# A gated mix of two long convolutions: one group moved back from the end to the middle of the run, the tap filter in wide multiplications, the gate by tanh

## The chip, the cores and the metric

One core of a Trainium2 chip. Its engines are PE (TensorE, matmuls; PEld is its loading of weights), DVE (VectorE), ACT (ScalarE), POOL (GpSimd) and SP (SyncE, which only issues DMAs here). Each has an in-order queue of its own, and they meet at semaphores. The metric is the device time of one execution in microseconds; the median of three runs is compared.

## The reference

```
g = sigmoid((u * gate_w).sum(-1, keepdims=True))
# A: a diagonal state space model as one long convolution per channel
K = einsum("dn,dnl,dn->dl", C, exp(dt * A * l), dt * B).real      # 448 channels, 256 modes, 2048 steps
a = causal_conv(u, K) + u * Dskip
# B: a gated convolution
k_shift = sum over t < 4 of k[s - t] * shift_k[:, t]              # the tap filter
kv = k_shift * v
b = u * (causal_conv(kv, ssm_k) + kv * ssm_D)
out = g * a + (1 - g) * b                                         # [1, 2048, 448], bf16
```

The convolutions are by FFT over 4096 points in the reference.

## The kernel before

**Layout.** The 2048 steps stand as 32 partitions of 64 steps, four times, once for each quarter of 112 of the 448 channels. So a tensor like `u`, `k` or `v` is a tile of 128 partitions x 64 x 112. The 112 columns are handled in four groups (`NQG = 4`, `NC = 28` columns each), for both convolutions: groups B0 to B3 and A0 to A3.

**One group.** A convolution is done as a Fourier transform by matmuls. `spread` (first stage, L215, PSUM tiles `ps_c`) and `transform` (second stage, L227, PSUM tiles `ps`) bring a tile `zs` into frequencies; each PSUM tile is brought to SBUF by a cast on ACT (`evac`, L567). A B group needs this for its filter (`KB`, from `skraw`) and for its data (`XB`, from `kv`); an A group for its data (`XA`, from `uu`) and for the generated kernel (`KA`, `zsK`). `swapped` (L605) makes a copy `zsS` with real and imaginary halves exchanged, by two DMAs on SP's queue. `products` (L286) multiplies both copies by the other factor, on DVE, two multiplications of 128x3584. `stage_a` (L265, `ps_a`, cast into `U`) and `stage_b` (L279, `ps_b`) transform back, and an epilogue on DVE puts the result into `ug`: L734 for B groups (`ug` holds u times 1-g by then), L744 and L746 for A groups. A2's result is held in `y` and mixed in later (`mix_y`, L764 and L765).

**The generated kernel.** K comes in eight blocks of 14 columns (`KGen.block(j)`, j = 0 to 7), two for each A group. A block is a chain of multiplications and additions on DVE that makes two tables of powers, `kg_TQ` and `kg_TP` (L320, L325, L330; the copy at L334 is among the first of each block), then 224 small matmuls `pk` (L373), a cast `kg_S` on ACT, a gather by matmuls (L414), two casts `kg_KT`, and a spread with `WcK` into `zsK`. Ahead of every second block `Tables.chunk(H)` makes the exponentials and phases for two blocks: ACT computes exponentials (L483, tiles `ks_mag` and `ET`) and sines (L495), which are in different tables, and DVE makes the phases (L491, `ks_ph`) and multiplies (L508). The queue order holds all sines of a chunk together and all exponentials together, by `after`.

**The front.** `k` is loaded into `kt` with three earlier steps ahead of it. The tap filter goes over 64 steps, eight at a time, from the last to the first: four multiplications on DVE (L653), each of eight steps of `kt` shifted by one step more, times that tap's row of `wt`, and then eight matmuls with the identity (L657), which add the four up in PSUM, and a cast back into `kt`. The matrices `A`, `B` and `C` come as `modes`, are transposed on PE (L447) and used at L436 and L455.

**The gate.** `ug` is first used for u times `gate_w` (L820), summed by matmuls (L823) and a reduction (L825); the sigmoid (L826) makes g in `gt`. `gb` holds g and `og` 1-g, and L832 makes `ug` = u times 1-g.

**The order.** `seq` says which group is convolved back in which step. `step(c, n, j)` brings in the next group n (spread, transform), takes the current group c back (stages A and B), and runs block j. A scheduler sets the order of instructions on each engine; `tc.high_priority` and `after` steer it. In this kernel B3 isn't in `seq`: its place is `None` (step 3 brings in nothing, step 4 takes nothing back), its spreads and transforms are written in the step of block 6, and its products, stages A and B come behind block 7. The last A group is done in two halves of 14 columns (`transform_half` L241, `last` L843, `stage_a_half` L253), each after one of the last two blocks; then stage B, the epilogue and the stores to `out` (L739).

Of the kernel before, what the change touches and what calls it, by code (L numbers as in the profile page):

```python
# [9 lines left out]
ACT = mybir.ActivationFunctionType  # L10
ALU = mybir.AluOpType
# [6 lines left out]
P = 128  # L18
# [4 lines left out]
NQG = 4  # L23
NC = 112 // NQG
CB = NC // 2
NBLK = 2 * NQG
# [25 lines left out]
def after(tc, ins, before):  # L52
    tc.add_manual_dep(ins.ins, before.ins.name,
                      mybir.DependencyInfo(mybir.DependencyClass.NoSync, mybir.DependencyReason.DATA),
                      reason="order on one engine")
# [6 lines left out]
class Consts:  # L62
# [67 lines left out]
    def stage_a(self, s_col, off_col):  # L130
        nc = self.nc
        j = self.iota("sa_j", [[1024, 64]])
        ph = self.carve(256).rearrange("p (i b) -> p i b", i=4)
        for i, off in enumerate((off_col[0][:, 0:1], off_col[1][:, 0:1], HALF, QUARTER)):
            self.phases(ph[:, i, :], j, s_col, off)
        R = self.pool.tile([P, 256], bf16, name="sa_R")
        nc.scalar.activation(R[:], low16(ph.rearrange("p i b -> p (i b)")), ACT.Sin, scale=PHASE)
        return R

    def stage_b(self, pool, qt, hqt, k_col, mask):  # L140
        nc = self.nc
        G = pool.tile([P, 64, 2, 4, 32], bf16, name="sb_G")
        jv = self.iota("sb_j", [[8, 16], [512, 32]]).rearrange("p (b a) -> p b a", b=16)
        offs = self.pool.tile([P, 4, 2], f32, name="sb_offs")
        for b0 in range(0, 64, 16):
            ph = qt([P, 16, 2, 32], "sb_ph", i32)
            for r, turn in enumerate((QUARTER, HALF)):
                o = offs[:, b0 // 16, r:r + 1]
                nc.vector.tensor_scalar(out=o, in0=k_col[:], scalar1=8.0 * b0, scalar2=turn, op0=ALU.mult, op1=ALU.add)
                self.phases(ph[:, :, r, :], jv, k_col, o)  # L150
            v = pool.tile([P, 16, 2, 32], bf16, name="sb_v", tag="kg_P4", bufs=2)
            nc.scalar.activation(v[:].rearrange("p b r a -> p (b r a)"), low16(ph[:].rearrange("p b r a -> p (b r a)")),
                                 ACT.Sin, scale=PHASE)
            for g in range(4):
                nc.vector.tensor_scalar(out=G[:, b0:b0 + 16, :, g, :], in0=v[:], scalar1=mask[:, g:g + 1], scalar2=None, op0=ALU.mult)
        return G
# [64 lines left out]
def transform(nc, psum, W, zs, evac, ks=range(4)):  # L221
    n = 4 * NC
    for kk in ks:
        pt = psum.tile([P, 2, 512], f32, name="ps_2", tag="ps")
        for i in range(8):
            k = 8 * kk + i
            nc.tensor.matmul(pt[:, i // 4, (i % 4) * n:(i % 4 + 1) * n], lhsT=W[:, k].rearrange("p r s -> p (r s)"), rhs=zs[:, k],  # L227
                             start=True, stop=True)
        evac(zs[:, 8 * kk:8 * kk + 8].rearrange("p (i k) c -> p i (k c)", i=2), pt[:, :, 0:4 * n], kk % 2)
# [50 lines left out]
        consume(b0, n, pt[:, :, 0:448])  # L280


def products(nc, X, S, Y, behind=None, k0=0, k1=32):
    fl = lambda t: t[:, k0:k1].rearrange("p k c -> p (k c)")
    for t in (S, X):
        op = nc.vector.tensor_tensor(out=fl(t), in0=fl(t), in1=fl(Y), op=ALU.mult)  # L286
        if behind is not None:
            behind(op)
    return X, S


# [236 lines left out]
def body(  # L528
# [20 lines left out]
    nc = tc.nc  # L549
    V = nc.vector  # L550
# [8 lines left out]
    qp = ctx.enter_context(tc.tile_pool(name="qp", bufs=NBQ))  # L559
    psum = ctx.enter_context(tc.tile_pool(name="psum", bufs=3, space=PSUM))  # L560
# [17 lines left out]
    def qt(shape, name, dtype=bf16):  # L578
        return qp.tile(shape, dtype, name=name, tag="q")
# [17 lines left out]
    def spread_in(cols):  # L597
        zs = qt([P, 32, 4 * NC], "zs")
        spread(nc, psum, Wc, zs, cols, [list(range(j, min(j + 8, NC))) for j in range(0, NC, 8)], evac)
        return zs  # L600

    def swapped(zs, op=None):
        swap = qt([P, 32, 4 * NC], "zsS")
        for r in range(2):
            d = nc.sync.dma_start(swap[64 * r:64 * r + 64], zs[64 - 64 * r:128 - 64 * r])  # L605
            if op is not None:
                behind_other(tc, d, op)
        return zs, swap

    kt = kgp.tile([P, 67, 112], bf16, name="kt", tag="kg_E")  # L610
# [4 lines left out]
    wraw = cons.carve(224).bitcast(bf16).rearrange("p (l t) -> p l t", t=4)  # L615
# [29 lines left out]
    ident = cons.carve(P // 2).bitcast(bf16)  # L645
    V.tensor_scalar(out=ident, in0=ji, scalar1=0.0, scalar2=None, op0=ALU.is_equal)
    wt = cons.carve(224).bitcast(bf16).rearrange("p (t l) -> p t l", t=4)
    wtc = nc.scalar.copy(wt, wraw.rearrange("p l t -> p t l"))
    for b0 in range(56, -1, -8):
        pt = psum.tile([P, 2, 512], f32, name="ps_v", tag="ps")  # L650
        t = qt([P, 4, 8, 112], "kvt")
        for n, tau in enumerate((3, 2, 1, 0)):
            V.tensor_tensor(out=t[:, n], in0=kt[:, b0 + 3 - tau:b0 + 11 - tau, :],  # L653
                            in1=wt[:, tau, :].unsqueeze(1).to_broadcast([P, 8, 112]), op=ALU.mult)
        for i in range(2):
            for n in range(4):
                nc.tensor.matmul(pt[:, i, 0:448], lhsT=ident, rhs=t[:, n, 4 * i:4 * i + 4, :].rearrange("p b l -> p (b l)"),  # L657
                                 start=(n == 0), stop=(n == 3))
        evac(kt[:, b0 + 3:b0 + 11, :].rearrange("p (i b) l -> p i (b l)", i=2), pt[:, :, 0:448])
# [4 lines left out]
    W2 = cons.stage_2(cons.field("b2", 0, 63), [cons.field("o2%d" % r, 6, 1, -QUARTER, (1 + r) * QUARTER) for r in range(2)], kgp, wtc)  # L664
    k_col, mask_b = cons.field("kB", 2, 31, 4.0, 1.0, pool=wp), cons.onehot("mgB", 4, cons.field("gB", 0, 3), 1.0 / 2048, pool=wp)
    R = cons.stage_a(cons.field("sA", 0, 63), [cons.field("oA%d" % r, 6, 1, HALF, (1 - r) * QUARTER) for r in range(2)])
    tb = Tables(tc, kgp, qt, hqt, psum, raw, ident, dt, xfd, nc.sync)
    tb.coefficients()
    G = cons.stage_b(kgp, qt, hqt, k_col, mask_b)
# [97 lines left out]
    def kv_cols(H):  # L767
        return lambda c: kvq[H][:, :, c]
# [1 line left out]
    def u_cols(H):  # L770
        return lambda c: uu[:, :, H * NC + c]

    def consume_a(c):
        with tc.high_priority(offset=300000):
            return stage_a(nc, psum, qp, R, terms[c], evac)

    def consume_b(c, U):
        with tc.high_priority(offset=200000):
            stage_b(nc, psum, G, U, (hold_y if c == ("A", NQG - 2) else epilogue_A if c[0] == "A" else epilogue_B)(c[1]))

    def step(c, n, j):
        kind, H = n if n else (None, None)
        if kind == "B":
            KB[H] = spread_in(skc.pop(H))
            XB[H] = spread_in(kv_cols(H))
        elif kind == "A":
            XA[H] = spread_in(u_cols(H))
        if c:
            U = consume_a(c)
        if kind == "B":  # L790
            transform(nc, psum, W2, KB[H], evac)
            transform(nc, psum, W2, XB[H], evac)
        elif kind == "A":
            transform(nc, psum, W2, XA[H], evac)
        if j == NBLK - 2:
            KB[3] = spread_in(skc.pop(3))
            XB[3] = spread_in(kv_cols(3))
            transform(nc, psum, W2, KB[3], evac)
            transform(nc, psum, W2, XB[3], evac)
        if c:  # L800
            consume_b(c, U)
        if kind == "B" and H + 1 < NQG:
            skc[H + 1] = sk_cols(H + 1)
        block(j)
        if kind == "B":
            with tc.high_priority(offset=200000):
                terms[n] = products(nc, *swapped(KB[H], kg.summed), XB[H])
        elif kind == "A":
            XA[H] = swapped(XA[H], kg.summed)
        if kind == "A" and H < NQG - 1:  # L810
            transform(nc, psum, W2, KA[H], evac)
            with tc.high_priority(offset=200000):
                terms[n] = products(nc, *XA[H], KA[H])
# [9 lines left out]
        nc.tensor.matmul(pg[:], lhsT=ones[:], rhs=ug[:, :, l:l + 8], start=(l == 0), stop=(l == 104))  # L823
    gt = wp.tile([P, 64], f32, name="gt")
    V.tensor_reduce(out=gt[:], in_=pg[:], op=ALU.add, axis=mybir.AxisListType.X)  # L825
    nc.scalar.activation(gt[:], gt[:], ACT.Sigmoid)  # L826
    gb = wp.tile([P, 64, 2], bf16, name="gb")
    V.tensor_copy(gb[:], gt[:].unsqueeze(2).to_broadcast([P, 64, 2]))
    og = wp.tile([P, 64, 2], bf16, name="og")
# [1 line left out]
    pairs = lambda t: t[:].rearrange("p b (n t) -> p b n t", t=2)  # L831
    V.tensor_tensor(out=pairs(ug), in0=pairs(uu), in1=og[:].unsqueeze(2).to_broadcast([P, 64, 56, 2]), op=ALU.mult)  # L832

    seq = [("B", 0), ("B", 1), ("B", 2), ("A", 0), None, ("A", 1), ("A", 2), ("A", 3)]
    for j in range(NBLK - 1):
        step(seq[j], seq[j + 1], j)

    KB[3] = swapped(KB[3], kg.summed)

    def last(half):  # L840
        for k0 in (0, 16):
# [3 lines left out]
    transform_half(nc, psum, W2, KA[3], evac, 0)  # L845
    last(0)
    block(NBLK - 1)
    terms["B", 3] = products(nc, *KB[3], XB[3], lambda op: after(tc, op, kg.last))
    consume_b(("B", 3), consume_a(("B", 3)))
    U = qt([P, 2, 64, NC], "U")  # L850
    transform_half(nc, psum, W2, KA[3], evac_two, 1)
    stage_a_half(nc, psum, U, R, XA[3], evac, 0)
    last(1)
# [38 lines left out]
```

## Time and profile before

| | us |
|---|---|
| median of three runs | 343.5 (341.89 to 343.77) |
| the profiled execution, its own time | 341.89 |
| its span, first to last instruction | 340.1 |
| busy: DVE / ACT / PE / PEld / POOL | 277.0 / 243.6 / 228.9 / 199.4 / 32.4 |
| mean granted TensorE clock | 0.817 |

The span is what the profile's rows lie in; the execution's own time is 1.8 us more. Starts are from the span's start. A row's duration has some 0.05 to 0.1 us that overlap the next row on the same engine, so sums over many instructions are made from start to start.

### The profile page before, as it was taken

Reading aid. Unit: us, or ns where it says so; the run is one execution under the profiler, and the core shown is the slowest. Engines: PE = TensorE matmul, PEld = TensorE weight load, DVE = VectorE, ACT = ScalarE, POOL = GpSimd, SP = SyncE. Lnnn points to the kernel's source line nnn. Section 1 sums busy time; section 2 is a strip of 40 time slices with the busy share of each in tenths; the row PEclk is TensorE's granted clock in tenths of the full one; section 3 lists DMA queues with packets and bytes.
Section 4 is the critical chain, followed back from the end, with each engine's and each line's share of the span. In section 5 each row is a group of like instructions: output and inputs, shape, how many; then the busy total and the mean of one; then the engine's idle time right before and its main releaser. Section 6 shows DMA issues by size and latency. Waiting matters only on the chain.

```text
span 340.1 us, 11947 instructions
## 1 busy us (share of the span) xinstructions
PE 228.9 (67%) x5286; PEld 199.4 (59%) x5286; DVE 277.0 (81%) x571; ACT 243.6 (72%) x395; POOL 32.4 (10%) x129
## 2 busy tenths in 40 slices
PE   0598325845497587799827887939759949847740
PEld 0145325345386486698717776839649848747740
DVE  7899999977997999799999999999999930171640
ACT  2745978599954899979768597889846837874320
POOL 9300003720000073000000000000000000000000
PEclk9999965678587679589958759678969997996995
DMA  5889999430002410500310100400040040400038
GB/s 112 141 186 154 162 164 194 165 54 0 2 2 57 90 24 5 150 2 4 83 30 4 44 3 5 110 0 4 16 95 5 4 110 4 110 2 0 4 76 142
DMA packets 53740, 21.41 MB, mean 63 GB/s; under 512 B 49080, under 2 KB 52024, under 8 KB 53688
## 3 DMA queue, kind: packets, MB, share of 16 engines
q1 hardware_dynamic: 48936, 19.47, 30.1%
q10 hardware_dynamic: 4560, 1.15, 1.9%
q8 instruction: 41, 0.67, 0.9%
q14 instruction: 11, 0.09, 0.1%
q0 software_dynamic: 192, 0.03, 0.1%
HBM read 10.09 MB, written 3.21 MB: 39 GB/s over the span
## 4 chain that ended last, share of the span: by engine, by line
DVE 40%; ACT 28%; PE 12%; SPq 6%; DMA 4%; issue 3%; POOL 3%; DVEq 0%; ACTq 0%
DVE kg_P L320 10%; ACT zs L567 9%; ACT ET L483 5%; PE ps_b L279 4%; ACT U L567 4%; DVE zs L286 3%; DVE zsS L286 3%; DVE kg_TQ L325 3%; DVE kg_TP L330 3%; DVE ks_ph L491 3%; DVE kg_TP L325 3%; POOL skraw L594 3%; ACT ks_mag L483 2%; PE pk L373 2%; PE ps_a L265 2%
## 5 line engine op out<-in xcount | busy, mean ns | idle before, releaser
L567 ACT CAST zs<-ps_c 128x1024 bf16<-128x1024 f32 (+1 forms) x48 | 41.6, 923 | 5.6 <-PE ps_c L215 5.6
L320 DVE TENSOR_TENSOR kg_P<-kg_TQ,ET 128x896 bf16<-128x896 bf16 (+1 forms) x64 | 43.8, 706 | 0.4
L227 PEld LDWEIGHTS <-s_W 128*128 128x128 bf16 x480 | 33.8, 117 | 16.1 <-issue 13.8
L567 ACT CAST zs<-ps 128x896 bf16<-128x896 f32 x48 | 40.7, 932 | 2.2 <-PE ps L227 2.2
L265 PE MATMUL ps_a<-sa_R,zs 128*128 128x128 bf16 x196 | 33.2, 263 | 12.1 <-DVE zs L286 7.8
L373 PE MATMUL pk<-kg_TP,kg_TQ 128*21 128x32 bf16 x1792 | 30.2, 238 | 12.1 <-issue 8.5
L227 PE MATMUL ps<-zs,s_W 128*128 128x112 bf16 x384 | 30.2, 242 | 11.7 <-ACT U L567 6.0
L373 PEld LDWEIGHTS <-kg_TQ 128*21 128x21 bf16 x1792 | 27.8, 121 | 13.8 <-issue 13.1
L567 ACT CAST U<-ps_a 128x1024 bf16<-128x1024 f32 (+2 forms) x32 | 28.8, 938 | 9.6 <-PE ps_a L265 7.4
L265 PEld LDWEIGHTS <-zs 128*128 128x128 bf16 x196 | 28.2, 156 | 8.8 <-DVE zs L286 8.3
L265 PE MATMUL ps_a<-sa_R,zsS 128*128 128x128 bf16 x196 | 32.7, 261 | 0.0
L279 PE MATMUL ps_b<-U,sb_G 128*128 128x28 bf16 x1024 | 27.6, 177 | 5.5 <-ACT U L567 3.7
L279 PEld LDWEIGHTS <-sb_G 128*128 128x128 bf16 x1024 | 27.5, 98 | 6.4 <-issue 6.2
L215 PE MATMUL ps_c<-WcK,kg_KT 128*64 128x128 bf16 x224 | 19.1, 298 | 17.7 <-ACT zsK L567 13.0
L320 DVE TENSOR_TENSOR kg_P<-kg_TP,ET 128x1792 bf16<-128x1792 bf16 (+1 forms) x32 | 30.9, 965 | 0.0
L265 PEld LDWEIGHTS <-zsS 128*128 128x128 bf16 x196 | 28.2, 157 | 4.4 <-issue 4.3
L594 POOL TENSOR_TENSOR skraw<-skraw,dB 128x28 bf16<-128x28 bf16 x4 | 21.1, 5277 | 97.8 <-DMA skraw<-in_B_ssm_k_dram 71.1
L215 PEld LDWEIGHTS <-kg_KT 128*64 128x64 bf16 x224 | 16.6, 209 | 20.2 <-issue 14.8
L325 DVE TENSOR_TENSOR kg_TQ<-kg_P 128x896 bf16<-128x896 bf16 (+2 forms) x64 | 27.8, 443 | 0.2
L495 ACT ACTIVATE ET<-ks_ph 128x448 bf16<-128x448 int16 x40 | 23.2, 590 | 6.6 <-DVE ks_ph L491 5.4
L567 ACT CAST zsK<-ps_c 128x512 bf16<-128x512 f32 (+2 forms) x28 | 21.4, 773 | 6.3 <-PE ps_c L215 6.2
L657 PE MATMUL ps_v<-kvt,scratch 128*128 128x448 bf16 x64 | 16.5, 397 | 13.3 <-DVE kvt L653 12.9
(141 smaller groups left out, 476.0 us busy)
## 6 DMA issues: line engine op xcount, KB each, us to landing
zsS<-zs SPq DMA_DIRECT2D x16, 448.0 KB, 5.6
kt<-in_B_k_dram SPq DMA_DIRECT2D x16, 112.0 KB, 4.3
skraw<-in_B_ssm_k_dram SPq DMA_DIRECT2D x16, 112.0 KB, 3.7
vt<-in_B_v_dram SPq DMA_DIRECT2D x4, 448.0 KB, 7.1
uu<-in_A_u_dram SPq DMA_DIRECT2D x4, 448.0 KB, 8.8
xfd<-ks_hold SPq DMA_DIRECT2D x2, 672.0 KB, 7.4
ks_xf<-xfd SPq DMA_DIRECT2D x3, 336.0 KB, 3.4
out_dram<-ug SPq DMA_DIRECT2D x8, 112.0 KB, 4.6
```

Source lines behind the costliest of these rows:

```text
L215: nc.tensor.matmul(pt[64 * r:64 * r + 64, i, :], lhsT=x, rhs=W[:, 128 * r:128 * r + 128], start=True, stop=True, tile_position=(0, 64 * r))
L227: nc.tensor.matmul(pt[:, i // 4, (i % 4) * n:(i % 4 + 1) * n], lhsT=W[:, k].rearrange("p r s -> p (r s)"), rhs=zs[:, k], start=True, stop= ...
L265: nc.tensor.matmul(pt[:, i, :], lhsT=t[:].rearrange("p k (g c) -> p (k g) c", g=4)[:, :, j + i], rhs=R[:, 128 * n:128 * n + 128], start=(n ...
L279: nc.tensor.matmul(o, lhsT=G[:, b, r].rearrange("p g a -> p (g a)"), rhs=U[:, r, b], start=(r == 0), stop=(r == 1))
L286: op = nc.vector.tensor_tensor(out=fl(t), in0=fl(t), in1=fl(Y), op=ALU.mult)
L320: put(V.tensor_tensor(out=P4[:, i:i + m].rearrange("p n v c m -> p n v (c m)"), in0=in0, in1=in1, op=ALU.mult))
L325: put(V.tensor_tensor(out=T[:, dst:dst + v.shape[1] // 2].rearrange("p n v m -> p (n v) m"), in0=v[:, :, 0], in1=v[:, :, 1], op=ALU.add))
L373: nc.tensor.matmul(pt[32 * g:32 * g + NQ, hw, :].rearrange("p (i j) -> p i j", i=2), lhsT=TQ[:, :, c, m], rhs=rhs, start=(hf == 0 and c == 0),
L483: ex = nc.scalar.activation(dst, x, ACT.Exp, scale=float(e))
L495: sn = nc.scalar.activation(dst.rearrange("p b c m -> p b (c m)"), low16(ph[:].rearrange("p b c m -> p (b c m)")).rearrange("p (b x) -> p ...
L567: return nc.scalar.copy(dst, src)
L594: nc.gpsimd.tensor_tensor(out=raw[:, :, 0], in0=raw[:, :, 0], in1=dB[:, H * NC:(H + 1) * NC], op=ALU.add)
```

## The change

Three things. The tap filter makes all four products of eight steps in one multiplication: its source reads `kt` with a step of 112 over four taps and again over eight steps, so that the reads overlap, and `wt` holds the taps in reverse order. The gate is computed as 0.5 + 0.5 tanh(x/2), placed behind the last exponential of the first chunk on ACT, with one more small operation on DVE. B3 stands in `seq` between A0 and A1: brought in with block 3, taken back with block 4; what was written for it at the end is taken out, with the order that it needed there.

```diff
-def products(nc, X, S, Y, behind=None, k0=0, k1=32):
+def products(nc, X, S, Y, k0=0, k1=32):
     fl = lambda t: t[:, k0:k1].rearrange("p k c -> p (k c)")
     for t in (S, X):
-        op = nc.vector.tensor_tensor(out=fl(t), in0=fl(t), in1=fl(Y), op=ALU.mult)
-        if behind is not None:
-            behind(op)
+        nc.vector.tensor_tensor(out=fl(t), in0=fl(t), in1=fl(Y), op=ALU.mult)
     return X, S
...
-    wtc = nc.scalar.copy(wt, wraw.rearrange("p l t -> p t l"))
+    wtc = nc.scalar.copy(wt, wraw.rearrange("p l t -> p t l")[:, ::-1])
     for b0 in range(56, -1, -8):
         pt = psum.tile([P, 2, 512], f32, name="ps_v", tag="ps")
         t = qt([P, 4, 8, 112], "kvt")
-        for n, tau in enumerate((3, 2, 1, 0)):
-            V.tensor_tensor(out=t[:, n], in0=kt[:, b0 + 3 - tau:b0 + 11 - tau, :],
-                            in1=wt[:, tau, :].unsqueeze(1).to_broadcast([P, 8, 112]), op=ALU.mult)
+        k0 = kt[:, b0:b0 + 8, :]
+        V.tensor_tensor(out=t[:], in0=bass.AP(k0.tensor, k0.offset, [list(k0.ap[0]), [112, 4], [112, 8], [1, 112]]),
+                        in1=wt.unsqueeze(2).to_broadcast([P, 4, 8, 112]), op=ALU.mult)
...
     def step(c, n, j):
-        kind, H = n if n else (None, None)
+        kind, H = n
         if kind == "B":
             KB[H] = spread_in(skc.pop(H))
             XB[H] = spread_in(kv_cols(H))
-        elif kind == "A":
+        else:
             XA[H] = spread_in(u_cols(H))
-        if c:
-            U = consume_a(c)
+        with tc.high_priority(offset=300000):
+            U = stage_a(nc, psum, qp, R, terms[c], evac)
         if kind == "B":
             transform(nc, psum, W2, KB[H], evac)
             transform(nc, psum, W2, XB[H], evac)
-        elif kind == "A":
+        else:
             transform(nc, psum, W2, XA[H], evac)
-        if j == NBLK - 2:
-            KB[3] = spread_in(skc.pop(3))
-            XB[3] = spread_in(kv_cols(3))
-            transform(nc, psum, W2, KB[3], evac)
-            transform(nc, psum, W2, XB[3], evac)
-        if c:
-            consume_b(c, U)
+        with tc.high_priority(offset=200000):
+            stage_b(nc, psum, G, U, (hold_y if c == ("A", NQG - 2) else epilogue_A if c[0] == "A" else epilogue_B)(c[1]))
...
-    nc.scalar.activation(gt[:], gt[:], ACT.Sigmoid)
+    after(tc, nc.scalar.activation(gt[:], gt[:], ACT.Tanh, scale=0.5), tb.exp)
+    V.tensor_scalar(out=gt[:], in0=gt[:], scalar1=0.5, scalar2=0.5, op0=ALU.mult, op1=ALU.add)
...
-    seq = [("B", 0), ("B", 1), ("B", 2), ("A", 0), None, ("A", 1), ("A", 2), ("A", 3)]
+    seq = [("B", 0), ("B", 1), ("B", 2), ("A", 0), ("B", 3), ("A", 1), ("A", 2), ("A", 3)]
     for j in range(NBLK - 1):
         step(seq[j], seq[j + 1], j)
 
-    KB[3] = swapped(KB[3], kg.summed)
+    U = qt([P, 2, 64, NC], "U")
...
     last(0)
     block(NBLK - 1)
-    terms["B", 3] = products(nc, *KB[3], XB[3], lambda op: after(tc, op, kg.last))
-    consume_b(("B", 3), consume_a(("B", 3)))
-    U = qt([P, 2, 64, NC], "U")
     transform_half(nc, psum, W2, KA[3], evac_two, 1)
```

More of the change, by code (lines that the diff above doesn't have):

```diff
@@ L771, in u_cols @@
         return lambda c: uu[:, :, H * NC + c]
[L773 to L779, printed above, removed]
     def step(c, n, j):
-        kind, H = n if n else (None, None)
+        kind, H = n
         if kind == "B":
@@ L807, in step @@
                 terms[n] = products(nc, *swapped(KB[H], kg.summed), XB[H])
-        elif kind == "A":
+        else:
             XA[H] = swapped(XA[H], kg.summed)
```

## The prediction

> **What bounds the kernel now.** I read the busy slices first (40 of 8.5 us, busy tenths), then VectorE's (DVE's) waits (sum in us, times, longest), then stretches cut at DVE's block starts (a row of line 334 marks each), then the rows of the tail. Slices:
>
> ```profile
> DVE  7899999977997999799999999999999930171640
> ACT   2745978599954899979768597889846837874320
> ```
>
> DVE's waits:
>
> ```profile
> DVE y L764 <- ACT y L567: 21.1, 2, 20.9
> DVE ug L734 <- PE ps_b L279: 11.2, 5, 8.4
> DVE ET L508 <- ACT ET L495: 5.7, 3, 2.4
> ```
>
> Stretches (start:end, length, then busy time and instructions of PE, PEld, DVE, ACT (ScalarE) and POOL, PE's granted clock, DMA):
>
> ```profile
> 154.00:185.00 31.00, 21.15 (x599) 19.52 (x601) 30.93 (x70) 24.95 (x41) 0.00 (x0) 0.83 0.15 33
> 185.00:204.00 19.00, 15.69 (x493) 14.59 (x481) 18.22 (x34) 14.57 (x35) 0.00 (x0) 0.68 0.09 22
> 204.00:234.00 30.00, 22.05 (x480) 20.08 (x477) 29.63 (x71) 25.27 (x39) 0.00 (x0) 0.75 0.14 33
> 275.00:340.10 65.10, 39.13 (x1041) 36.68 (x1040) 18.19 (x26) 29.63 (x38) 0.00 (x0) 0.86 0.29 57
> ```
>
> From slice 10 to slice 32 DVE is full: the middle is DVE's. The last 65 us are not: DVE works 18.2 of 65.1 us. In the three middle stretches DVE is idle 0.07, 0.8 and 0.4 us, ACT 6.0, 4.4 and 4.7 us. So work put there costs its DVE time in full and its ACT time only beyond about 15 us.
>
> The rows of DVE in the tail say what fills it (start, duration, engine, line, operation, and in brackets the idle time before it and what ended it):
>
> ```profile
> 273.77 1.09 DVE L330 TENSOR_TENSOR kg_TP<-kg_TP,ET 128x1792 bf16<-128x1792 bf16 x1
> 295.73 0.62 DVE L764 TENSOR_TENSOR y<-y,gb 128x896 bf16<-128x896 bf16 x1 [20.87 <-ACT y L567]
> 303.19 2.02 DVE L286 TENSOR_TENSOR zsS<-zsS,zs 128x3584 bf16<-128x3584 bf16 x1
> 315.51 1.09 DVE L734 TENSOR_TENSOR ug<-ps_b,ug 128x896 bf16<-128x896 f32 x1 [8.37 <-PE ps_b L279]
> ```
>
> And two rows of PE:
>
> ```profile
> 280.88 0.63 PE L373 MATMUL pk<-kg_TP,kg_TQ 128*21 128x32 bf16 x29 [2.86 <-issue]
> 316.93 0.99 PE L241 MATMUL ps<-zsK,s_W 128*128 128x56 bf16 x32
> ```
>
> Block 7 leaves DVE at 274.9 us. Then comes group B3, almost serially: spread casts 273.4 to 275.4 and 282.5 to 288, transforms to 294.5, products 303.2 to 307.1 (L286), stage A to 313.7, stage B to 317.1. That is 2.0 + 12.0 + 13.9 = 27.9 us. Only behind it does PE start the last half transform of A3 (316.93), from which the end is 23.2 us away.
>
> **The change, part by part.** I make the sum in this one execution: span 340.1 us, its own time 341.9 us, median of three runs 343.5 us. The difference of spans is then added to the median.
>
> *Tap filter (L653).* Out go 32 multiplications of 128x896, 17.1 us from 11.7 to 28.8 us, 0.535 us each. In come 8 of 128x3584. The same shape is in the trace as L286, 1.94 us from start to start, and L320, which also reads with broadcasts and odd strides, keeps the rate (128x1792 in 1.00 us). So 15.5 us: 1.6 us off DVE. But PE can't begin on a quarter of the result any more: 8 matmuls instead of 5 follow the last multiplication (5 took 1.11 us), and in the changed program's instruction order all transposes of `modes` (L447) follow them, where 16 went between before. DVE and ACT need those at L436 and L455. I put the filter's gain at 33 us at 0.2 us, and at nothing after that, because the second `skraw` addition of POOL starts at 56.75 us, behind DMAs whose issue does not depend on DVE, and holds back PE to 66.3 us. Bounds: 1.6 us gained to 1 us lost.
>
> *Gate.* The rows of ACT:
>
> ```profile
> 66.96 1.01 ACT L567 CAST zs<-ps_c 128x1024 bf16<-128x1024 f32 x1 [0.98 <-PE ps_c L215]
> 69.37 1.28 ACT L826 ACT_TABLE_LOAD   x1
> 71.40 1.28 ACT L495 ACT_TABLE_LOAD   x1
> 80.06 1.28 ACT L483 ACT_TABLE_LOAD   x1
> ```
>
> And DVE's rows that wait for ACT's sines:
>
> ```profile
> 78.84 0.40 DVE L508 TENSOR_TENSOR ET<-ET,ks_mag 128x448 bf16<-128x448 bf16 x1 [2.20 <-ACT ET L495]
> 109.04 0.39 DVE L508 TENSOR_TENSOR ET<-ET,ks_mag 128x448 bf16<-128x448 bf16 x1 [2.37 <-ACT ET L495]
> ```
>
> From 66.96 to 80.06 us ACT has no gap, and DVE waits for it (2.20 us) before block 0 can start at 80.6. The change takes out two table loads (2.56 us; the new order has none for the tanh) and the sigmoid (0.17), and the order moves two casts (0.90 + 0.46) behind the exponentials: block 0 starts 4.1 us earlier (bounds 2.6 and 4.5). The price: the multiplication of `ug` by 1-g (L832, 3.85 us), which ran under that ACT stretch, now stands inside block 0 with three small ones (0.3 us): 4.15 us, and up to 0.6 us of wait, since L812 of the changed kernel waits for the tanh on ACT with all of block 0 queued behind it. Together: nothing (1.5 us either way).
> The Trainium skill, page "ScalarE: Activation LUTs", section "Table sets: the hidden batching unit", puts a table load at about 2.7 us; by that the two loads would be 5.4 us, but the rows say 1.28 each.
>
> *Order on ACT.* At 106.58 ACT's `kg_S` cast, waiting for PE, stands ahead of the sines of the next chunk, and DVE pays 2.37 us at 109.04; in the new order two sines stand ahead of it: 1.9 us gained (0 to 2.4). DVE's 1.87 us wait for `ps_b` at 142.7 us has more work before it: 1.0 us (0 to 1.9).
>
> *B3 in blocks 3 to 5.* DVE takes on two products (2 x 1.94, L286) and two epilogue multiplications (2 x 1.08, L734): 6.0 us, all on the path. ACT takes on 8 spread casts (6 of 0.90, 2 of 0.46), 8 transform casts (0.80), 4 of U (3.2 in all): 15.9 us. Counting the instructions between two `kg_S` casts, ACT then has 32.5 us for block 3 against DVE's 32.3 us, 7.7 against 14.9 in block 4, 31.4 against 38.3 in block 5. So ACT fits over the three, but in block 3 without any slack, and its queue is in order: the `kg_S` cast of block 4 waits for PE, which has B3's transforms and A0's stage B ahead of that block's matmuls; behind it stand block 5's sines. The products wait for two swap DMAs (5.6 us to landing). I take 3 us of new waits (0, if it goes as in the stretches above, to 13, if of ACT's 15.1 us of idle time the 15.9 us can use only 3).
>
> *Tail.* B3's 27.9 us leave it. What is late next is block 7's own chain. From DVE's end of block 7: matmuls of `pk` 6.0 us (they took 3.6 in block 2 and 6.6 in block 7; now stage B of A2, 3.4 us, and the spread of block 6 stand ahead of them); `kg_S` 0.53; four half casts 1.84; two KT casts and a gather 0.55 + 0.62 + 0.58; spread and its casts 3.2 (302.4 to 305.6); and from the half transform to the end 23.2, as before. Sum 36.5 us, where it was 340.1 - 274.9 = 65.2: 28.7 us less. Bounds 34 and 39.
> Within it stage A of A3 was fast: its 28 matmuls ran 0.064 us apart (318.5 to 320), while B3's ran 0.106 us apart at 307.3 to 309. With no dense B3 work before it the slower pace may hold: 28 x 0.042 = 1.2 us, part of the upper bound.
> The Trainium skill speaks against this part: "TensorE: Matmul & The Clock Gate", Part 1, says the array is throttled by default and is released after some 3.4 us of busy time. By that rule both half stages would be slow, and the tail 2.4 us longer, an estimate.
>
> *Sum.* DVE's end of block 7: 274.9 - 0 (filter) + 0 (gate) - 2.9 (order) + 6.0 + 3.0 = 281.0. End: 281.0 + 36.5 = 317.5, that is 22.6 us less. Median: 343.5 - 22.6 = 320.9, said as 321 us.
>
> **Rivals.**
> - *ACT becomes the bound in blocks 3 to 5.* For it: 32.5 against 32.3 us in block 3. Against: the counts of blocks 4 and 5, and block 1, which had 26.9 us of ACT in 34.3 us and cost DVE 2.4 us. Price: 13 instead of 3 us: 331 us.
> - *The wide multiplication loses the double rate*, because its source overlaps itself. The f32 source of L734 shows a slower rate: 128x896 in 1.00 us from start to start against 0.535. For 3584 that is 4.0 us less three times the overhead of some 0.07: 3.8 us, 1.9 us more each. 8 x 1.9 = 15 us more on DVE, of which the start of POOL at 56.75 hides 2: 334 us. For it no row; against it L320's odd strides.
> - *B3 goes serially in the middle, and the kernel gets slower.* Mechanism: ACT's in-order queue. If every cast of B3 stands where DVE waits for it, the 27.9 us of the tail come back, with the 5.6 us of swap that the tail hid: 33.5 instead of 9.0 us, 345.4 us. It gets slower by over 0.5% only when the middle stretches by more than 33.3 us. Against it: DVE has block work to do in all that time, which it had not in the tail.
> - *It doesn't do what it says* has no case: both orders show 8 multiplications, no sigmoid load, and B3's products between blocks 4 and 5.
>
> **How the numbers follow.** Forecast 0.73; ACT as the bound 0.16; lost rate 0.05; serial 0.05; 0.01 for an end near no change. A measurement of this kernel tells about 0.5% (1.7 us) from no change. Faster: 0.73 + 0.16 + 0.05 = 0.94, less 0.01 for mixtures of the rivals: 0.93. Slower is the serial case, 0.05; the same gets that 0.01 and the 0.01 near no change, 0.02. The forecast's own range is 314 (front and order at their best, no new waits) to 328. To leave out no more than 2 in 10 it goes up through ACT as the bound, with a slow tail: 313 to 334.
>
> **What would show it.** Right: 8 multiplications of 1.9 us; block 0 at some 76.5 us; DVE full until about 281, then idle some 13 us except for `y` and the first half of A3; half transform near 294. Wrong: multiplications of 3.8 us; DVE waits for ACT's sines in blocks 3 to 5 of over 8 us together; or a tail from DVE's end of block 7 of more than 39 us.

## The result, and the profile after

The changed kernel takes 327.56 us (median of four runs, 327.22 to 329.9) beside 342.69 us (341.7 to 343.77) for the kernel before on the same chip: a ratio of 0.957, with an interval of 0.951 to 0.963. That is 15.1 us less where 22.6 were forecast; the forecast of 321 us is 6.6 us short, and its range of 313 to 334 us holds the result. The profiled execution has a span of 325.5 us (own time 327.3), 14.6 less than before, where the sum of the prediction ends at 317.5: in spans it is 8.0 us short.

The busy slices of the changed kernel, 40 of 8.1 us (busy tenths):

```profile
DVE  7898999958899999989999969879999869942440
ACT  2645888689991799979899997199999555936600
```

DVE is nearly full from slice 10 to slice 34 now (the first slice is 0), and the hollow tail is five slices long where it was eight. But in the middle there are 6, 7 and 8 where the kernel before, from slice 17 on, had only nines. ACT has a hole there too: the 1 in slice 25 is the `kg_S` cast of block 4, which waits 8.45 us for `pk` before 209.85 us. DVE's waits in the changed kernel (sum in us, times, longest):

```profile
DVE zsS L829 <- ACT zsK L565: 7.2, 1, 7.2
DVE ET L506 <- ACT ET L493: 6.1, 5, 1.7
DVE ept L742 <- PE ps_b L279: 5.7, 2, 4.4
DVE zsK L571 <- ACT zsK L569: 5.5, 1, 5.5
DVE zsS L286 <- ACT zsK L565: 2.8, 1, 2.8
DVE kg_TP L343 <- PE pk L371: 2.5, 1, 2.5
DVE zsS L286 <- DMA zsS<-zs: 1.8, 1, 1.8
```

The 20.9 us for `y` and the 8.4 us for `ps_b` are gone; 7.2 and 5.5 us are block 7's own chain in the tail. The last three rows are new and lie in the middle, and so do 1.7 us of the sines and 1.3 us of `ept`: 10.1 us in blocks 4 to 7. (Lines of the changed kernel are 2 lower than before up to about L760, and 14 to 17 lower behind that.)

Stretches of the changed kernel, from block start to block start on DVE for blocks 3 to 7, and the tail (start:end, length, then busy time and instructions of PE, PEld, DVE, ACT and POOL, PE's clock, DMA):

```profile
149.19:181.74 32.55, 27.30 (x759) 24.88 (x762) 32.45 (x72) 30.58 (x49) 0.00 (x0) 0.95 0.13 31
181.74:199.54 17.80, 13.51 (x340) 12.10 (x329) 15.20 (x31) 17.31 (x37) 0.00 (x0) 0.81 0.14 33
199.54:241.61 42.07, 35.08 (x1036) 32.51 (x1033) 38.47 (x78) 32.96 (x54) 0.00 (x0) 0.84 0.18 43
241.61:259.73 18.12, 15.20 (x306) 13.84 (x307) 16.72 (x32) 14.80 (x27) 0.00 (x0) 0.80 0.20 45
259.73:285.83 26.10, 23.49 (x613) 21.71 (x612) 23.28 (x38) 17.92 (x23) 0.00 (x0) 0.88 0.07 17
285.83:325.50 39.67, 20.08 (x575) 18.61 (x573) 12.09 (x23) 13.10 (x18) 0.00 (x0) 0.68 0.35 66
```

DVE leaves block 7 at 285.83 us, 39.67 us before the end. Blocks 3 to 7 take 136.6 us, of which DVE is busy 126.1 us. In the kernel before the same five blocks took 121.4 us (153.44 to 274.86) with 119.3 busy. So the middle grew by 15.2 us: 6.9 of work and 8.4 of idle time. Of the work 6.0 is B3's; about 1.0 is one multiplication of a B group's epilogue (`ug` from `ps_b`) that stood in block 2 before and stands in block 3 now. The tail shrank by 25.6 us, from 65.2.

### The profile page after: what moved, and what is told of

The parts are those of the page before. It is cut to its first block, busy times and chain, and to the rows that moved or that the text cites. A ratio compares the mean times of both kernels' runs of the same rounds, so it can differ in the third digit from the quotient of the medians.

```text
span 325.5 us, 11920 instructions
## 1 busy us (share of the span) xinstructions
PE 225.0 (69%) x5286; PEld 198.1 (61%) x5286; DVE 275.4 (85%) x548; ACT 239.8 (74%) x393; POOL 30.8 (9%) x129
## 4 chain that ended last, share of the span: by engine, by line
ACT 34%; DVE 19%; PE 18%; SPq 14%; DMA 6%; issue 3%; POOL 3%; DVEq 0%; ACTq 0%; POOLq 0%
ACT zs L565 10%; ACT zsK L565 6%; ACT ET L481 6%; DVE kg_P L318 6%; PE ps_b L279 4%; PE ps_c L215 4%; SPq L587 4%; PE pk L371 4%; SPq L634 3%; ACT U L565 3%; ACT ET L493 3%; POOL skraw L592 3%; SPq L631 3%; SPq L619 2%; PE ps L227 2%
## 5 line engine op out<-in xcount | busy, mean ns | idle before, releaser
L565 ACT CAST zs<-ps_c 128x1024 bf16<-128x1024 f32 (+1 forms) x48 | 42.1, 931 | 3.2 <-PE ps_c L215 3.2
L565 ACT CAST zs<-ps 128x896 bf16<-128x896 f32 x48 | 41.4, 930 | 1.1 <-PE ps L227 1.0
L227 PEld LDWEIGHTS <-s_W 128*128 128x128 bf16 x480 | 33.0, 116 | 11.9 <-issue 10.2
L592 POOL TENSOR_TENSOR skraw<-skraw,dB 128x28 bf16<-128x28 bf16 x4 | 19.5, 4880 | 96.8 <-DMA skraw<-in_B_ssm_k_dram 96.8
L655 PE MATMUL ps_v<-kvt,scratch 128*128 128x448 bf16 x64 | 14.5, 381 | 15.2 <-DVE kvt L651 14.2
L215 PE MATMUL ps_c<-WcK,kg_KT 128*64 128x128 bf16 x224 | 19.9, 305 | 6.0 <-ACT zsK L565 4.2
L215 PE MATMUL ps_c<-Wc,kv 128*64 128x128 bf16 x224 | 15.9, 323 | 11.1 <-DVE kv L680 8.0
```

The source lines that it names most:

```text
L215: nc.tensor.matmul(pt[64 * r:64 * r + 64, i, :], lhsT=x, rhs=W[:, 128 * r:128 * r + 128], start=True, stop=True, tile_position=(0, 64 * r))
L565: return nc.scalar.copy(dst, src)
L592: nc.gpsimd.tensor_tensor(out=raw[:, :, 0], in0=raw[:, :, 0], in1=dB[:, H * NC:(H + 1) * NC], op=ALU.add)
```

## The experiments

Ratios are to the kernel before, measured beside each run, with their intervals. "DVE's end" is where DVE leaves block 7, and the tail runs from there to the end of the span. Both are read from one execution of each kernel: three kernels that differ from each other only behind that point, in block 7's own chain (the changed one, `e19_halfpk`, `e9_tail`), have it at 285.8, 286.9 and 287.2 us, so a difference of about 1 us there says nothing. In the order of the square: which of the three edits brings the time?

**B3's move alone** (`e1_b3`): the changed kernel with the old filter and the old gate.

```diff
-        V.tensor_tensor(out=t[:], in0=bass.AP(...overlapping...), in1=wt...to_broadcast([P, 4, 8, 112]), op=ALU.mult)
+        for n, tau in enumerate((3, 2, 1, 0)):
+            V.tensor_tensor(out=t[:, n], in0=kt[:, b0 + 3 - tau:b0 + 11 - tau, :], in1=wt[:, tau, :]..., op=ALU.mult)
...
-    after(tc, nc.scalar.activation(gt[:], gt[:], ACT.Tanh, scale=0.5), tb.exp)
-    V.tensor_scalar(out=gt[:], in0=gt[:], scalar1=0.5, scalar2=0.5, op0=ALU.mult, op1=ALU.add)
+    nc.scalar.activation(gt[:], gt[:], ACT.Sigmoid)
```

> The kernel before with group B3 moved into the middle and nothing else: four tap multiplications per eight columns and the Sigmoid are kept. Theory (the whole gain is B3's: the tail loses some 25 us, the middle grows by some 11): 327.5 us, within 1.5 of the changed kernel; block 0 starts on DVE at 80.7 us, DVE leaves block 7 at 284 to 287 us, 39 to 40 us before the end. Rival (filter and gate bring 3 us or more of the 15): 330.5 us or more, with DVE leaving block 7 at 289 us or later. Second rival (the 2.4 us sine wait at 109 us and the 1.9 us wait at 142.7 us went because of the gate's new place on ACT and not because of B3): both waits are back, 2 to 4 us.

Measured: 326.23 us, ratio 0.951 (0.948 to 0.954). B3's move alone brings 17.2 us, no less than all three edits together. DVE's end is 284.8, the tail 39.2 us. The five stretches of blocks 3 to 7 in this kernel:

```profile
152.72:184.85 32.13, 27.86 (x759) 25.72 (x761) 31.54 (x71) 29.64 (x44) 0.00 (x0) 0.89 0.14 32
184.85:200.04 15.19, 9.33 (x295) 8.17 (x285) 15.09 (x31) 15.18 (x38) 0.00 (x0) 0.89 0.24 56
200.04:242.43 42.39, 38.68 (x1016) 36.60 (x1019) 38.69 (x77) 36.51 (x55) 0.00 (x0) 0.88 0.15 36
242.43:262.20 19.77, 11.90 (x358) 10.50 (x347) 18.25 (x35) 13.92 (x30) 0.00 (x0) 0.72 0.21 49
262.20:284.82 22.62, 21.77 (x604) 20.45 (x604) 21.76 (x35) 17.02 (x22) 0.00 (x0) 0.94 0.09 18
```

They take 132.1 us with 125.3 busy: 10.7 us more than before, 6.1 of work and 4.6 of waits. The second rival held: with the old gate both waits are back, the sine wait with 1.44 us (at 108.27) and the `ps_b` wait with 1.91 (at 141.98), 3.35 together where 2 to 4 were expected. So B3's move is not what took the sine wait away.

**The front alone** (`e2_front`): the kernel before with the wide filter and the tanh, B3 at the end.

> The kernel before with the wide tap multiplication and the tanh gate, and B3 left at the end. Theory (the two together are worth nothing): 342.7 us within 1.5; block 0 starts at some 76 us, block 1 at some 96 us, as in the changed kernel, because the 3.85 us multiplication of ug now stands inside block 0. Rival (they bring 3 us or more): 339.7 us or less. If the order on ACT (sines ahead of a kg_S cast) comes from the gate, 339.8 us, with the sine wait at 109 us under 0.5 us.

Measured: 339.64 us, ratio 0.988 (0.985 to 0.992). The theory fell: the front alone brings 3.8 us. DVE's block starts (copy at L334) in this kernel:

```profile
76.09 0.21 DVE L334 COPY kg_TQ<-ET 128x224 bf16<-128x224 bf16 x1
96.44 0.22 DVE L334 COPY kg_TQ<-ET 128x224 bf16<-128x224 bf16 x1
127.87 0.23 DVE L334 COPY kg_TQ<-ET 128x224 bf16<-128x224 bf16 x1
```

Block 0 starts 4.8 us earlier than before, block 1 0.4 later: that part is worth nothing, as forecast. Block 2 then starts 2.5 us earlier, since the sine wait at 109 us is gone. So that gain needs no B3; it is there in the kernels with the tanh (block 2 at 127.8 to 128.0 us) and not in those with the sigmoid (129.6 to 130.4), so it belongs to the gate's new place in ACT's queue. DVE's end is 272.6 us, 2.2 us earlier.

**The other two corners** (`e3_nogate`: the changed kernel with the old gate; `e4_nofilter`: with the old filter).

> The changed kernel with the Sigmoid back in its old place: wide tap multiplication and B3 in the middle stay. Theory (the gate trades 4.5 us of earlier start for 4.2 us inside block 0): 327.6 us within 1.0, block 0 at 80.5 us and block 1 at 96 us. Rival (the gate helps by taking two table loads out of a full ACT): 329.6 us or more.

> The changed kernel with the four tap multiplications back; tanh gate and B3 in the middle stay. It fills the last corner of the square: B3 alone 326.2, B3 with the wide filter 326.9, all three 327.6 us. Theory (the gate's earlier start is eaten in blocks 4 to 7 by the order on PE and ACT, the filter does nothing): 327 to 328 us. Rival (the two front edits cost only together): 325 us or less, the front's gain of 2 to 3.7 us kept.

Measured: 326.87 us, ratio 0.952 (0.949 to 0.954), and 329.34 us, ratio 0.961 (0.959 to 0.963). With B3 in the middle the corners are 326.2 (neither), 326.9 (filter), 329.3 (gate) and 327.6 us (both): nothing that the front gains is left. The filter's direct effect is small: block 0 starts at 80.80 with it and 80.97 without (old gate), 76.05 and 76.21 (new gate), 0.16 us each time. The rival of `e4_nofilter` fell. The gate alone is even slower than neither (the intervals lie apart); the 1.8 us between it and all three can't be told from chance, and neither can the 1.3 us between neither and all three, since those intervals overlap.

**Is ACT the bound in the middle?** (`e11_act8`)

```diff
+    def twice(dst, src, i=0):
+        evac(dst, src)
+        return evac(dst, src)
...
-            transform(nc, psum, W2, KB[H], evac)
-            transform(nc, psum, W2, XB[H], evac)
+            transform(nc, psum, W2, KB[H], twice if H == 3 else evac)
+            transform(nc, psum, W2, XB[H], twice if H == 3 else evac)
```

> The changed kernel with every cast of B3's two transforms made twice on ACT (the second writes the same values): 8 casts of 0.80 us more in block 3 and 4, 6.4 us of ACT. Theory (ACT is not the bound, it stands idle at kg_S and sines for 31 us over the kernel): the end moves by at most 2 us, 329.6 us or less. Rival (ACT is the bound in these blocks, the prediction's first rival): the end moves by most of 6.4 us, 332 to 334 us.

Measured: 329.54 us, ratio 0.964 (0.958 to 0.970): 2.0 us more for 6.4 us of ACT (the profile has 8 more instructions on ACT and 7.0 us more of busy time), the theory's bound. And DVE's end came at 283.4 us, 2.4 earlier than in the changed kernel, while the tail grew to 43.7. So that much more work on ACT costs DVE nothing here; the order of all queues behind block 4 changed with it (block 5 takes 36.2 us in place of 42.1), so it isn't shown that ACT never holds DVE up. What the run loses is in the tail, where DVE waits for `y`:

```profile
292.45 0.62 DVE L766 TENSOR_TENSOR y<-y,gb 128x896 bf16<-128x896 bf16 x1 [8.95 <-ACT y L565]
```

**Is DVE the bound in the middle?** (`e23_noprod`: B3's two products left out.)

```diff
-                terms[n] = products(nc, *swapped(KB[H], kg.summed), XB[H])
+                pair = swapped(KB[H], kg.summed)
+                terms[n] = products(nc, *pair, XB[H]) if H < 3 else pair
```

> The changed kernel with B3's two products of 128x3584 left out of the middle (2 x 1.94 us of DVE; stage A then reads the pair as it is). Theory (DVE is the bound in the middle, so B3's DVE work is on the path in full): 3.9 us less, 323.7 us, more by 1.8 us if the wait for the swap DMA ahead of them goes with them. Rival (ACT's and PE's queues are the bound in blocks 3 to 7): 326.5 us or more, with new waits in place of the products.

Measured: 330.83 us, ratio 0.964 (0.961 to 0.967). With 3.9 us of work less it isn't faster. DVE's end came at 283.0, 2.9 us earlier, and the tail took 44.1 us. PE's stage B of A2 and DVE's wait for it in this kernel:

```profile
292.22 3.36 PE L279 MATMUL ps_b<-U,sb_G 128*128 128x28 bf16 x128
...
295.01 0.63 DVE L762 TENSOR_TENSOR y<-y,gb 128x896 bf16<-128x896 bf16 x1 [11.97 <-ACT y L565]
```

The same stage in the changed kernel:

```profile
281.66 3.36 PE L279 MATMUL ps_b<-U,sb_G 128*128 128x28 bf16 x128 [0.26 <-ACT zs L565]
```

There it is done before DVE leaves block 7; here PE has it behind block 7's `pk`, and the time that DVE saved comes back in the tail. The theory failed; the rival's time came (326.5 us or more), but not in its form: part of DVE's saving did reach DVE's end (2.9 of 3.9), and the end of the kernel didn't follow.

**Is it PE's order?** `pk` has the lower priority than stages A and B. In the changed kernel block 3's `pk` runs in four pieces, with stage A of a neighbour between them, and DVE waits behind it:

```profile
180.78 1.49 PE L371 MATMUL pk<-kg_TP,kg_TQ 128*21 128x32 bf16 x87 [1.36 <-DVE kg_TP L328]
...
185.99 0.24 PE L371 MATMUL pk<-kg_TP,kg_TQ 128*21 128x32 bf16 x3
...
187.81 0.92 PE L371 MATMUL pk<-kg_TP,kg_TQ 128*21 128x32 bf16 x48
...
189.31 1.49 PE L371 MATMUL pk<-kg_TP,kg_TQ 128*21 128x32 bf16 x86
...
190.84 0.22 DVE L343 COPY kg_TP<-ET 128x224 bf16<-128x224 bf16 x1 [2.50 <-PE pk L371]
```

With B3's move alone the same block's `pk` is one piece, and DVE has no wait there:

```profile
183.89 3.54 PE L371 MATMUL pk<-kg_TP,kg_TQ 128*21 128x32 bf16 x224 [0.73 <-DVE kg_TP L328]
```

Two runs raise `pk`'s priority above the stages, in every block (`e10_pkfirst`) and in block 3 alone (`e17_pk3`):

```diff
-        with self.tc.high_priority(offset=100000):
+        with self.tc.high_priority(offset=400000):                              # e10_pkfirst
+        with self.tc.high_priority(offset=400000 if j == 3 else 100000):        # e17_pk3
             pt = self.pk...
```

> The changed kernel with the priority of the pk matmuls of every block raised above those of stages A and B, so that TensorE takes a block's 224 pk matmuls as soon as DVE has finished the block. Question: the middle grew by 15.2 us from block 3 to block 7 where 9 were forecast, and DVE waits 2.5 us at 190.8 us for pk of block 3, while ACT stands 8.45 us before 209.85 us at the kg_S cast. Theory (the order on PE: pk stands behind stage A and stage B of the neighbours, and ACT's in-order queue stands behind the kg_S cast): the wait of 2.5 us goes and part of the sine and product waits with it (1.7 and 2.75 us): 322 to 325 us. Rival (those stages are needed just as early, by the epilogues on DVE): their ps_b waits grow by as much, 327.5 us or more.

> The changed kernel with the priority of the pk matmuls raised in block 3 alone (raised in every block it gave 340.8 us). In the changed kernel block 3's 224 pk matmuls run in four pieces (87, 3, 48 and 86) from 180.8 to 190.8 us, with stage A of a neighbour between them that waits for ACT; in the kernel with B3's move alone they run in one piece of 3.5 us, and DVE has no wait there. Theory (the pieces are what eats the gate's gain of some 2 us, by the wait of 2.5 us at 190.8 us): that wait goes and the end comes 1 to 2.5 us earlier, 325 to 326.5 us. Rival (stage A is wanted as early as pk, the wait only moves to the products of B3 or to the epilogues): 327.5 us or more.

Measured: 340.79 us, ratio 0.996 (0.993 to 0.999), and 331.51 us, ratio 0.967 (0.964 to 0.969). The theory fell twice, the rival held. The wait at 190.8 us went both times, and came back elsewhere. In `e10_pkfirst`, for the swap of B3 and for A2's result:

```profile
206.09 2.02 DVE L286 TENSOR_TENSOR zsS<-zsS,zs 128x3584 bf16<-128x3584 bf16 x1 [5.33 <-DMA zsS<-zs]
...
301.79 0.63 DVE L762 TENSOR_TENSOR y<-y,gb 128x896 bf16<-128x896 bf16 x1 [9.71 <-ACT y L565]
```

DVE's end is 292.0 us there, 6.2 later than in the changed kernel, and the tail 48.7, 9.0 longer. Some 4.7 us of the tail (an estimate, 6.6 less 1.04 and 0.81 us, by the rows below) have a cause of their own: the new order lets PE take the second half of block 6's spread and the start of block 7's gather in turns, one matmul each. The first half of the spread in one piece, and two of the turns:

```profile
302.39 1.04 PE L215 MATMUL ps_c<-WcK,kg_KT 128*64 128x128 bf16 x14
...
305.12 0.33 PE L215 MATMUL ps_c<-WcK,kg_KT 128*64 128x128 bf16 x1
305.38 0.22 PE L412 MATMUL ps_g<-kg_S,ga_sel 128*32 128x112 bf16 x1
305.53 0.33 PE L215 MATMUL ps_c<-WcK,kg_KT 128*64 128x128 bf16 x1
```

The 14 matmuls of the spread and 17 of the gather take 6.6 us so (303.37 to 309.97), each turn 0.41 to 0.51 us; in one piece each they take 1.04 (the row above) and 0.81 us (the changed kernel, from 295.07). The first half transform of the tail (310.98) waits for the cast of that spread.

In `e17_pk3`, four waits of blocks 5 and 6:

```profile
206.55 2.03 DVE L286 TENSOR_TENSOR zsS<-zsS,zs 128x3584 bf16<-128x3584 bf16 x1 [2.28 <-DMA zsS<-zs]
216.54 0.39 DVE L506 TENSOR_TENSOR ET<-ET,ks_mag 128x448 bf16<-128x448 bf16 x1 [2.31 <-ACT ET L493]
...
243.14 2.03 DVE L286 TENSOR_TENSOR zsS<-zsS,zsK 128x3584 bf16<-128x3584 bf16 x1 [2.14 <-ACT zsK L565]
...
260.57 1.09 DVE L742 TENSOR_TENSOR ept<-ps_b,gt 128x896 bf16<-128x896 f32 x1 [2.63 <-PE ps_b L279]
```

Block 5 starts 1.8 us earlier than in the changed kernel (197.76), DVE's end comes 3.6 us later (289.4).

**B3 one place earlier** (`e5_pos3`)

```diff
-    seq = [("B", 0), ("B", 1), ("B", 2), ("A", 0), ("B", 3), ("A", 1), ("A", 2), ("A", 3)]
+    seq = [("B", 0), ("B", 1), ("B", 2), ("B", 3), ("A", 0), ("A", 1), ("A", 2), ("A", 3)]
```

> The changed kernel with B3 one place earlier: B0, B1, B2, B3, A0, A1, A2, A3 in place of B0, B1, B2, A0, B3, A1, A2, A3. Theory (B3's DVE work is on the path wherever it stands in the middle, and the waits depend on the order that ACT and PE get): the tail stays at 39 to 40 us, the middle moves by up to 3 us either way: 325 to 330 us. Rival (blocks 2 and 3 already have B2's casts on ACT, and two groups B in a row overload it): 331 us or more, the waits in blocks 2 and 3.

Measured: 334.61 us, ratio 0.979 (0.976 to 0.982): the rival's time, but not at its place. The waits of 2.2 to 3.3 us are in blocks 5 and 7 (A groups' products at 213.4 and 281.6 us, an epilogue at 263.7), and the tail is 42.8 us with A2's stage B behind block 7's `pk`.

**The path of the spreads** (`e7_ps4`: `if j >= NBLK - 2` becomes `NBLK - 4`) and **DVE's share of the last casts** (`e9_tail`: the second KT cast and the second spread cast of block 7 on DVE).

> The changed kernel with the spreads of blocks 4 and 5 on the path that blocks 6 and 7 have (two groups of 7 columns through the three PSUM buffers that all others use, in place of four groups through one buffer of their own). Theory (the products of A2 wait 2.75 us at 266.9 us since PE and ACT take turns at the single buffer, some 0.7 us each, before the transform casts): the casts are two of 1.05 us in place of four of 0.6 us, the wait shrinks by 1 to 2 us: 326 us. Rival (the spreads then take PSUM buffers from the stages, whose casts come late): 328 us or more.

> The changed kernel with DVE taking half of the casts of block 7's own chain: the second KT cast and the second spread cast, both idle time of DVE. Theory (in the tail ACT's casts stand one behind the other on the path, and the tail is 3.2 us over the forecast partly there): the chain from the kg_S cast to the half transform (8.1 us) shortens by 0.9 us for the spread and up to 0.5 us for KT: 326.3 us. Rival (DVE's casts wait for the same matmuls, and the path is PE's): 327.6 us, no change. If the half stage then runs more at the slow clock (0.106 instead of 0.064 us apart) part of it is given back: 327.0 us.

Measured: 327.52 us, ratio 0.958 (0.954 to 0.961), and 328.15 us, ratio 0.955 (0.952 to 0.959): no change from either. In `e7_ps4` the 2.8 us product wait shrank to 0.45, the others did not, a new one of 1.6 us for `pk` stands in block 7, and DVE's end is where it was (0.5 us later). In `e9_tail` the way from `kg_S` to the half transform takes 8.0 us in place of 8.1: two casts side by side gain little, since PE hands over the second only 0.8 us after the first.

**What `pk` costs in the tail** (`e19_halfpk`: half of block 7's `pk` left out)

```diff
-                    for c in range(2):
+                    for c in range(1 if j == NBLK - 1 else 2):
```

> The changed kernel with half of block 7's pk matmuls left out (the imaginary parts: 112 instead of 224), nothing else moves. In the tail pk takes 6.7 us, of which 2.85 us are waits for issue between pieces of 94, 128 and 2. Theory (these waits are TensorE's instruction supply, which falls behind after 256 instructions in a row without a pause): with half the instructions the waits shrink with the work, pk takes 1.9 to 3.2 us, the tail shortens by 3.5 to 4.8 us: 323 to 324 us. Rival (the waits have another cause that stays, only the matmul time of 3.9 us is halved): the tail shortens by 1.9 us, 325.6 us.

Measured: 323.87 us, ratio 0.945 (0.943 to 0.948); the tail is 35.8 us, 3.9 less. Block 7's `pk` in the changed kernel:

```profile
286.75 1.59 PE L371 MATMUL pk<-kg_TP,kg_TQ 128*21 128x32 bf16 x94
289.57 2.10 PE L371 MATMUL pk<-kg_TP,kg_TQ 128*21 128x32 bf16 x128 [1.23 <-issue]
293.30 0.23 PE L371 MATMUL pk<-kg_TP,kg_TQ 128*21 128x32 bf16 x2 [1.62 <-issue]
```

And with half of it:

```profile
287.45 1.64 PE L371 MATMUL pk<-kg_TP,kg_TQ 128*21 128x32 bf16 x94
290.26 0.47 PE L371 MATMUL pk<-kg_TP,kg_TQ 128*21 128x32 bf16 x18 [1.18 <-issue]
```

6.8 us became 3.3. The matmuls themselves are 3.9 us (1.59 + 2.10 + 0.23) and 2.1, so 1.8 us of the 3.5 are theirs. The rest are waits for issue, in which PE waits for nothing that the profile shows: the first stays at its place behind the 94th matmul, the second, 128 matmuls on, has no instructions left to stand before. The theory's time came, and the waits sit at fixed places in the sequence of instructions. That they are TensorE's instruction supply isn't shown by it.

## Why the prediction was right or wrong

The mechanism holds: B3's move is the gain (17.2 us alone). Two terms were too small: the new waits in the middle (by 5.4 us) and the tail (by 3.2 us). With them the result of 327.6 us lies nearer to the first rival's 331 than to the forecast's 321, though not by that rival's cause, as far as the rows and `e11_act8` show.

**Filter: right.** Eight multiplications in 15.6 us (two pairs of rows: 11.69 for six, 3.94 for two), so no lost rate, and that rival is out. Next to nothing of it arrives behind the front: POOL's second `skraw` addition starts at 56.96 us (56.75 before) and ACT's cast behind it at 66.84, 0.12 us earlier. The prediction has DMAs ahead of that addition; the profile of before puts its start down to PE (`ps`), that of the changed kernel to a DMA, in neither case to DVE.

**Gate: right in itself.** The rows of the changed kernel:

```profile
76.05 0.21 DVE L332 COPY kg_TQ<-ET 128x224 bf16<-128x224 bf16 x1
82.98 0.19 DVE L812 TENSOR_SCALAR gt<-gt 128x64 f32<-128x64 f32 x1 [0.89 <-ACT gt L811]
85.28 3.88 DVE L818 TENSOR_TENSOR ug<-uu,og 128x7168 bf16<-128x7168 bf16 x1
96.40 0.21 DVE L332 COPY kg_TQ<-ET 128x224 bf16<-128x224 bf16 x1
```

Block 0 starts 4.8 us earlier (4.1 forecast, at most 4.5), pays 3.9 for `ug` and 0.9 for the wait (at most 0.6 forecast), and block 1 starts 0.3 us later than before: nothing, as the sum had it. From 66 to 90 us ACT now has one table load, 1.28 us at 75.56, and none for the tanh. The Trainium skill, page "ScalarE: Activation LUTs", section "Table sets: the hidden batching unit", says that an exponential and a tanh share one load; this trace agrees, but the load is 1.28 us here and about 2.7 us on the page.

**Order on ACT: right.** Forecast 2.9 us; block 3 starts 4.25 us earlier than before (2.9 in block 1, 1.7 in block 2, less the 0.3 of the gate). But 1.0 of block 2's share is the multiplication that moved into block 3, so 3.2 us are gained. `e2_front` shows the same 2.9 in block 1, and the same move, without B3.

**B3 in the middle: the term that fell short.** The forecast added 6.0 us of work and 3 us of new waits to DVE, and took the order's gain off in full. The work came as forecast. The new waits of blocks 3 to 7 are 8.4 us, inside the bounds (0 to 13) but 5.4 more than the 3 in the sum. With B3 alone they are 4.6 us, and the sum for blocks 3 to 7 is close: 10.7 us measured, 9 forecast. The rest comes when the front is changed too: its gain doesn't come on top. By the square, the front is worth 3.8 us without B3 in the middle and nothing (-1.3 us, not told from zero) with it. DVE's end is 285.8 in place of 281.0: 5.2 us worse in the middle, 0.35 better by the order.

The first rival had 13 us of waits, nearer in size, but its sign did not come: DVE's waits for sines in blocks 3 to 5 are 1.7 us, where over 8 would have shown it, and `e11_act8` adds 6.4 us of ACT to B3's 15.9 without moving DVE's end back. What the runs show in its place is that the order on the queues decides, beside the amount of work on any of them. PE is busy 114.6 of 136.6 us in blocks 3 to 7 (91.8 of 121.4 before), and takes `pk`, stages, transforms and spreads in one queue; with B3 alone it is as busy (109.5 of 132.1), so its load by itself doesn't explain the waits that the front adds. Three edits that leave all work as it is and change what is placed or ranked (`e5_pos3`, `e10_pkfirst`, `e17_pk3`) cost 4.0 to 13.2 us, and the one that takes 3.9 us of DVE's work away gains nothing. In four runs A2's stage B, or most of it, stands behind block 7's `pk` (`e5_pos3`, `e10_pkfirst`, `e11_act8`, `e23_noprod`), and the tail is 42.8 to 48.7 us in place of 39 to 41; in the last two of them DVE had come through 2.4 and 2.9 us earlier, and lost that and more. The forecast worked with a DVE sum to block 7 and a fixed tail behind it; the two are not independent.

What stays open: which of the queues would have to be reordered to keep the front's 2 to 4 us. Each change gives PE, ACT and DVE another order from the scheduler in blocks 4 to 7, so a run can't hold the order and take away one wait. A second buffer for `kg_TP` (14 KB more in each partition) might remove the wait at 190.8 us without a change of priority; it wasn't tried.

**Serial in the middle: out.** `e10_pkfirst` (340.8 us) isn't that case, since more of its loss is in the tail (9.0 us) than ahead of it (6.2); but it shows how little it takes: one number in a priority takes back 13 of the 15 us.

**Tail: right in its steps, short by 3.2 us.** It takes 39.7 us, past the bound of 39 that the prediction gave as a sign of being wrong. From DVE's end to `kg_S` 7.7 us (6.0 forecast), from there to the half transform 8.1 (7.3), from there to the end 23.8 (23.2). The largest miss is `pk`, with two waits for issue of 1.2 and 1.6 us. The half transform is slow (1.65 us, 0.99 before), and of stage A's two halves the first runs 0.106 us a matmul (303.13 to 305.99), the second 0.064 from 307.0 on. The profile's granted clock shows it: 1.00 up to 289 us, 0.50 from 290 to 306, 0.99 from 306.9 on. The fall (289.9 us) comes just behind `pk`'s first wait for issue, and between 282 and 307 us PE never pauses for more than 1.7 us. The Trainium skill, page "TensorE: Matmul & The Clock Gate", Part 1, has the array throttled by default and released after some 3.4 us of busy time. By that the forecast had an estimate of 2.4 us more; the rows show one slow half and one fast, half of that price. The release comes some 5 us after PE's last pause of over 1 us, so this trace agrees with the rule in kind and doesn't show its 3.4 us.

## What to carry to other kernels

Gains on an engine that is full need not add up: before B3 moved, 2 us less on ACT's path to DVE reached the end; afterwards new waits in blocks 4 to 7 absorbed it. So after each edit read again which stretch is bound by what, and weigh a second edit against the kernel that has the first in it. Where a scheduler sets the order, a small edit can reorder three queues, and single edits (one at a time, and left out one at a time) say more than a sum of parts; here one of three edits gave the whole gain.

## What was not expected of the hardware

The same 224 small matmuls of `pk` take 3.5 us in one place (block 3 with B3's move alone, the row shown above) and 6.8 us in another (block 7 of the changed kernel), the difference being waits for issue inside. Over all blocks and runs that were looked at, those without such waits took 3.5 to 3.7 us where nothing else stood between them, those with them up to 7.8 us (block 7 of `e10_pkfirst`, one wait of 4.0 us). Wherever two such waits fall into one block's `pk` (16 blocks in the profiles of all kernels here), exactly 128 matmuls lie between them, and each has a weight load of its own: 256 instructions. `e19_halfpk` shows that a wait whose place is not reached is not paid; the profile's instruction queue moved 0.67 MB in 41 packets, 16 KB each (divided). That PE waits for its instructions to arrive fits all of this, but no run shows it directly, and why one run of 224 has the waits and another hasn't stays open.

Nor were two other things. In `e10_pkfirst` matmuls of two shapes taken in turns need 0.41 to 0.51 us a pair, where in one piece each they need some 0.12 (0.074 and 0.048 us a matmul, divided). And in the tail of the changed kernel the granted clock falls to half without any pause of PE above 1.7 us.
